# A gated mix of a state-space convolution and linear attention: its last attention output block emitted in two steps, and a new table for the order of all work

## The chip, the cores and the metric

The kernel runs on one core of a Trainium2 chip. The metric is device time in microseconds (us), the median of three runs: 252.57 us before the change (251.17 to 252.98). The engines are named as the profile names them: PE (TensorE, matrix products into PSUM), DVE (VectorE), ACT (ScalarE), POOL (GpSimd) and SP (SyncE, which here only issues transfers). "SPq" and "ACTq" are the queues of transfers that SP and ACT issue.

## The reference

One input x (2048 tokens of 512 channels) goes through two branches and is mixed by a gate:

```python
x = A_u
g = sigmoid((x * gate_w).sum(-1, keepdims=True))
a = _A_ref(x, ...)      # long convolution of each channel with a kernel K of 2048 taps, + u * Dskip
b = _B_ref(x, ...)      # 32 heads of 16; phi = [softmax(p), softmax(-p)] of q and k; linear attention; @ wo
return g * a + (1 - g) * b
```

K of branch a is the real part of a sum over 128 complex exponentials of each channel, K[d,l] = Re sum_n C[d,n] exp(dt A[d,n] l) dt B[d,n]. The convolution is a product of spectra (FFT of 4096 points). In branch b, kv sums phi_k times v over all tokens, z sums phi_k, and the output is (phi_q kv) / (phi_q z + 1e-6), times wo. The result is 2048 by 512 in bf16.

## The kernel before, in words

The kernel doesn't emit instructions directly. It records some thousand *nodes* (`P.add(engine, name, function, deps, ...)`, and `P.dma` for transfers), and `Plan.run` then emits them in the order of a table, `ORDER`: two base-64 digits for each node. Every engine executes its instructions in the order in which they were emitted, so the table sets the order on each engine. Three other tables go with it: `SIDES` says for each copy out of PSUM that may run on ACT or DVE which of them does it, `RINGS` from which of two PSUM pools a matmul's result takes its buffers (each of the big pools has two buffers), and `WARM`, `FOURS`, `ZPS` hold variants that the change leaves alone. A name in the text such as zk or kn is the name of a node. Transfers share eight completion semaphores: a transfer waits until the last one that used its semaphore has landed, whichever queue that was on.

The work has these stages, with the lines of the profile:

- Start. Weights and x are transposed on PE and copied out by ACT and DVE (xps to xT, wtp to wT, wps to WW and Wqp). The node p_e computes exp(log_dt) (ACT, `pt<-ld`, line 96), and the nodes p_t multiply parameters by it on DVE (`ppx<-psri`, line 347). The nodes udc copy x once more (`UDp<-UD`); the first stage of the input's FFT (psAu, line 517, its result copied by XAu) needs all four copies.
- Keys, eight rounds of two token tiles each: pk (PE, line 635) makes the keys, ek (ACT, `Ek<-pk`, line 96) two exponentials of each, zk (DVE, `Zk<-Ek`, line 662) their sums, rz (ACT, `Zk<-Zk` and `vr<-Zk`) the reciprocal as a logarithm and an exponential, vp (PE, line 683) the values, vb their copy out of PSUM, vr (DVE, line 692) the scaled values, and kn (PE, `kvp<-vr,Ek`, line 700) adds the round to kv. The FFT of the input (psAu and XAu, then psBu, line 542, and XU, `xst<-psB`) is woven into the rounds.
- Tables: between the rounds and after them DVE and ACT fill the tables of the exponentials (Ctab, Dtab), ACT with a sine table. argC (PE, `args<-selE,statC`, line 953) and cs (ACT, `cs<-args`) make the sines of four units at a time, argE and E the exponentials, El, Rh, Rl, A1, A2, A3 (DVE, lines 989, 1054, 1058, 1037, 1042, 1047) the factors of K of one unit (32 channels; sixteen units), and kps (PE, line 209) multiplies them. There is one buffer for A, so A1 of a unit waits for kps of the unit before.
- Queries (pq, eq, zs, z1 to z5, em, ops, oT, in four blocks of 512 tokens), woven into the units.
- The convolution of 128 channels at a time, then of 64, 32 and 32: psA and XA, psB and XK (FFT of K), t (DVE, line 1230, product of the spectra), psz and Zr (back), zw and zr (a turn through DRAM), psy (PE, line 1319) and ou (DVE, lines 1328 and 1330), which multiplies by the gate and writes into xT; from there the stores `out` (line 1341).
- The end: block 3 of the attention output, which adds the convolution's share Y, goes through bpsL (PE, lines 876 to 879), bs3 and bsg (copies, lines 177, 911 and 913) to the stores outL (line 925). bpsL makes two token tiles, k = 0 and 1, in one node:

Of the kernel before, what the change touches and what calls it, by code (L numbers as in the profile page):

```python
# [98 lines left out]
class Plan:  # L99

    DIGITS = "0123456789abcdefghijklmnopqrstuvwxyzABCDEFGHIJKLMNOPQRSTUVWXYZ-_"
    ORDER = ("0001021d0x0y0z0o0p0q0G0H0I0f0g0h0D0E0F170i0j0k181415162z2C0304051h2E0l0m0n0607082F0u0v0w2D0r0s0t2G2I2K1e1f090a0b1C2H0c0d"
             "0e1g2M1A1i1j1k0A0B0C1r2L2N2O2J1D1s102P11121t131L0-1E1u1v1w2S1M0_1B2Q2T2R1N1F1I0Y2U1b0Z1G2V1J191a2W0J0K0L0M0N0O0P0Q0R0S0T"
             "0U0V0W0X1c1S2X4n202Y2Z4u4v4w2A2-4x4J2_304y4K4L4M31324B4F4z4A4C1H4N344G4D334Q4E4H4I4Y1P4R364O354Z4U371K4P1R4S4-4V4_533839"
             "542B4T504W1X1O571Y4X513a525b3C585c3c5d5e59555i3b5j563d5a5f5q5r5g3h5m1U5s3i5h5t5k5x3D5n3j5o5l5u5y3e3f3g5B5p1Z5F5v5C3k5w3o"
             "5H5z5G5D5M5A5I3q1T5E215J3E3p5Q1V5R5K4o5N5L5U1Q3r3l3m3n4p1l1m1n5O1x1y1z1-5W3v3x5V5S3y5P3F1W3w5X5T67693G4q683I5Y6a3H6b3J5Z"
             "3K6c3M1o1p1q5-6d3L3N3s3t3u3O1_235_3P223Q3R25243S3U3T2b272d3V263W2c3z3A3B2f3X2h2e28632j2i3Y3Z3-3_402g2l412k43442s2u482942"
             "2t2m4a2n4b2o454647492p4f2q4c4d4e2w2r2v4h2a2x6064612y4i4g656e874r6i628b6f6j4j4k4l6g6686858a6k4m6h6l886r6m7x898c4s8d8e6t6q"
             "8h8i4t8j8f8n8g6u7y8k8l8B8o8t8p6v6w6s8C6-8m6x8q6y8u6_70718r9_8Y8Z8-8H6z8s6A6B72748v8D7z8Ia06n6o6p756C736D9293948w8K8E8F6E"
             "8L8x8y6F6G6H768M8G8z778Q787B8A7C8J6I6J6K8Ra8796M6N6O7a7A8N8Oa97b9R8P8S9Va19W6Laaa26P9S8T7D9X7c7d7e9U9Z8U6Qa5a36Sa68W8Vae"  # L110
             "a48X9Ta79Y6Tam7f7g7h9-6U6Ranaf7i6W7Eabac98as8_9091ad996X9a7F9g7Gag6V7n7H9h7Iao7j7k7lbSah7JbT7patavaw9b9i7K9596977m9c9j9k"
             "7L7M7Nap9o9paBaxbI9w9x6YaibMbNajakbJaqal6Z9q7r7O7P7QbO7S7T7U7oar7qauaC7RbL7sbQay9y7t7Waz9l9m9naA7YbK7u7vaD7ZaPaQaR7VbPb_"
             "7X7-bR7w80aEc0aMaNaOaFaHbYaG9r817_82bUbV9d9e9fc1bWbZbXaIaVc59s83aJaKaL9z84b1cm9t9u9vaWb-9AaXb2aYc6c2cnaSaTaUb9coaZdJc3ba"
             "cscddLdKc4ceb3ctbba-a_b0c7dM9B9C9DeFc8bhcgdNeGb4cfdO9E9F9Gb5cjbidPbcchdQdRbd9Kckcic9dS9Lewcbca9MclexeHcpdzccdDekelem9N9H"
             "9I9J9OdEcqbebfbgdCdHcrbjcubkdTdUdVcvblcwb6b7b89PcxeCcycAcBcCczdBeydWdXdY9QezcMeDd-d_e0dZeAcUeBcNcOe1cVbmbnbocDcEcFdAeEdF"
             "dGeIeLcPcWeJcGcHcIbpbqbreMd0d1eKdId2bvcXcQcYd8cJcKcLbwfld9eNcRcScTfmbxcZc-c_eOd3fGePd4dafobsbtbueRdbeQe2eSbyfndcfpeTe3bz"
             "fHeUe4e_e5freneoepf0fqbAfsd5d6d7dmbBdddedfeVeteuevdgdhdieWfMf1fteXfuf2fvdnfIf3fJdjdkdleYeZe-fNf4f5f6fKfLeqeresfwdpfxdqfy"
             "drdofOfPdsfQe6fRdtdudve7f7f8f9fSfTfafbfcfzeafAfUebe8fXdwdxdye9fBfVfYfWfCf-ecfdbCbDbEfZedbFbGbHg0fDfEfef_g1g2g3eeefegehei"
             "ejfffgfhfifjfkfFg4g5g6g7g8g9gagbgc")
# [1472 lines left out]
```

## Time and profile before

| | |
|---|---|
| median of three runs | 252.57 us |
| profiled execution, its own time | 253.07 us |
| its span (first to last instruction) | 251.3 us |
| DVE busy | 224.1 us (89%) |
| ACT busy | 210.7 us (84%) |
| PE busy | 203.6 us (81%) |
| mean share of the granted PE clock | 0.956 |

The profiled execution's own time is 1.8 us above its span, and 0.5 us above the median. In the views, a row of the timeline has the start, the duration, the engine, the line, the operation with `out<-in`, the shapes and how many instructions follow each other in that row; in square brackets stands the engine's idle time before the row and what ended it. Consecutive instructions of an engine overlap a little: DVE rows of 1.22 us follow each other every 1.13 us, ACT rows of 1.02 us every 0.91 us. In the view of windows each engine has its busy time and, in brackets, its instructions in the stretch; PEclk is the granted share of the PE clock.

### The profile page before, as it was taken

To read this page: it belongs to the slowest core of one execution; us is meant where nothing else is said; L and a number is where in the kernel's file an instruction comes from. 1 tells how busy PE (TensorE), PEld (TensorE's weight loads), DVE (VectorE), ACT (ScalarE), POOL (GpSimd) and SP (SyncE) were. 2 spreads that over 40 slices of the span, in tenths; PEclk is the share of its full clock that TensorE was granted. 3 is DMA by queue.
4 is the path that set the end of the run, shared out by engine and by line. 5 is a ranking of instruction groups with operands and counts; after the bars stand their busy time and mean duration, and the time that the engine had idled before them with its cause. 6 is when DMAs were issued, how large, how long until landed. Compare 5 with 4: busy or idle time off the path is not lost.

```text
span 251.3 us, 9877 instructions
## 1 busy us (share of the span) xinstructions
PE 203.6 (81%) x4437; PEld 141.7 (56%) x4437; DVE 224.1 (89%) x287; ACT 210.7 (84%) x291; POOL 2.4 (1%) x7
## 2 busy tenths in 40 slices
...
GB/s 132 262 180 195 411 12 4 109 106 118 84 222 0 170 210 288 93 3 23 180 69 202 60 50 223 284 3 125 172 208 195 199 208 231 246 191 140 209 181 92
DMA packets 61922, 38.23 MB, mean 152 GB/s; under 512 B 40632, under 2 KB 57272, under 8 KB 61496
## 3 DMA queue, kind: packets, MB, share of 16 engines
...
HBM read 24.49 MB, written 13.11 MB: 150 GB/s over the span
## 4 chain that ended last, share of the span: by engine, by line
ACT 30%; PE 28%; DVE 22%; DMA 11%; issue 5%; SPq 2%; ACTq 0%; DVEq 0%
ACT cs L96 6%; PE pk L635 4%; ACT Eq L96 4%; PE vp L683 4%; DMA Zd<-Zr 3%; PE psB L542 3%; ACT E L96 3%; DVE t L1230 2%; DMA wqk<-in_B_wqkv_dram 2%; ACT XA L175 2%; ACT L93 2%; DMA XUd<-xst 2%; PE kps L209 2%; DMA ax<-apd 2%; DMA ZT<-Zd 2%
## 5 line engine op out<-in xcount | busy, mean ns | idle before, releaser
L209 PE MATMUL kps<-R,A 128*32 128x64 bf16 x1664 | 30.5, 228 | 2.7 <-DVE A L1042 0.8
L209 PEld LDWEIGHTS <-A 128*32 128x32 bf16 x1664 | 28.6, 160 | 7.3 <-issue 3.9
L96 ACT ACTIVATE cs<-args 128x1024 bf16<-128x1024 f32 x32 | 30.7, 1054 | 0.0
L1058 DVE TENSOR_TENSOR R<-E,cs 128x2048 bf16<-128x2048 bf16 x16 | 19.5, 1217 | 0.0
L1037 DVE TENSOR_TENSOR A<-Ctab,Dtab 128x2048 bf16<-128x2048 bf16 x16 | 19.5, 1218 | 0.0
L1042 DVE TENSOR_TENSOR A<-Ctab,Dtab 128x2048 bf16<-128x2048 bf16 x16 | 19.5, 1217 | 0.0
L1054 DVE TENSOR_TENSOR R<-E,cs 128x2048 bf16<-128x2048 bf16 x16 | 19.5, 1217 | 0.0
L175 ACT CAST Zr<-psz 128x1024 bf16<-128x1024 f32 (+1 forms) x17 | 16.5, 974 | 3.2 <-issue 1.2
L175 ACT CAST XK<-psB 128x1024 bf16<-128x1024 f32 (+1 forms) x15 | 15.0, 1009 | 4.3 <-PE psB L222 2.8
L542 PE MATMUL psB<-XAu,TB 64*128 64x128 bf16 x256 | 12.8, 262 | 6.9 <-ACT xst L175 4.8
L175 ACT CAST XA<-psA 128x1024 bf16<-128x1024 f32 (+1 forms) x16 | 15.6, 1006 | 3.2 <-PE psA L216 3.2
L683 PE MATMUL vp<-WW,xT 128*128 128x512 bf16 x64 | 18.0, 411 | 0.0
L1230 DVE TENSOR_TENSOR t<-XUX,XK 128x2048 bf16<-128x2048 bf16 x14 | 17.1, 1218 | 1.0 <-ACT XK L175 1.0
L96 ACT ACTIVATE Ek<-pk 128x512 bf16<-128x512 f32 x32 | 16.9, 601 | 0.4 <-PE pk L635 0.2
L96 ACT ACTIVATE Eq<-pq 128x512 bf16<-128x512 f32 (+1 forms) x28 | 16.7, 710 | 0.2 <-PE pq L769 0.2
L96 ACT ACTIVATE E<-args 128x1024 bf16<-128x1024 f32 x16 | 16.8, 1057 | 0.0
L542 PEld LDWEIGHTS <-TB 64*128 64x128 bf16 x256 | 10.3, 116 | 11.0 <-issue 10.8
L1256 PE MATMUL psz<-t,small 128*128 128x512 bf16 x60 | 15.2, 380 | 1.6 <-ACT cs L96 0.5
L769 PE MATMUL pq<-xT,Wqp 128*128 128x512 bf16 x64 | 15.6, 380 | 0.6 <-ACT Eq L96 0.6
L635 PE MATMUL pk<-WW,xT 128*128 128x512 bf16 x64 | 16.0, 380 | 0.0
L662 DVE TENSOR_REDUCE Zk<-Ek 128x64 f32<-128x1024 bf16 x12 | 14.0, 1208 | 0.0
L222 PE MATMUL psB<-XA,TB 128*128 128x128 bf16 (+2 forms) x160 | 9.6, 205 | 4.3 <-ACT XA L175 1.4
...
## 6 DMA issues: line engine op xcount, KB each, us to landing
...
```

The costliest lines, as they stand in the source:

```text
L96: return self.nc.scalar.activation(**kw)
L175: self.nc.scalar.copy(out=o, in_=i)
L209: nc.tensor.matmul(kps[32 * dj:32 * dj + 32, g4, e, :], lhsT=A[:, ka, :, :, d].rearrange("p a b -> p (a b)"), rhs=R[:, kr, d, :], start=(i ...
L542: nc.tensor.matmul(box.ps[:, c2, sl, :], lhsT=fc.TB[rows, b0:b0 + 2].rearrange("p a b -> p (a b)"), rhs=X.t[rows, k, r0 + sl].rearrange("p ...
L635: nc.tensor.matmul(box.ps[:], lhsT=xT[:, st, kt, :], rhs=g.WW[:, kt, :], start=(kt == 0), stop=(kt == 3))
L683: nc.tensor.matmul(box.ps[:], lhsT=xT[:, st, kt, :], rhs=g.WW[:, 4 + kt, :], start=(kt == 0), stop=(kt == 3))
L769: nc.tensor.matmul(box.ps[:, m - m0, :] if late else box.ps[:], lhsT=g.Wqp[:, kt, 128 * m:128 * m + 128], rhs=xT[:, 4 * b:4 * b + 4, kt, : ...
L1037: nc.vector.tensor_tensor(out=c.A[:, 0:2].rearrange("p o a b c -> p (o a) b c"), in0=g.C[U // 8][:, 0:2, :, d0 % 256:d0 % 256 + 32].rearra ...
L1042: nc.vector.tensor_tensor(out=c.A[:, 2:4].rearrange("p o a b c -> p (o a) b c"), in0=g.C[U // 8][:, 1:3, :, d0 % 256:d0 % 256 + 32].rearra ...
L1054: nc.vector.tensor_tensor(out=c.R[:, :, :, 32:64], in0=t.E[:, 1].unsqueeze(1).to_broadcast([128, 2, 32, 32]), in1=t.cs[:], op=ALU.mult)
L1058: nc.vector.tensor_tensor(out=c.R[:, :, :, 0:32], in0=t.E[:, 0].unsqueeze(1).to_broadcast([128, 2, 32, 32]), in1=t.cs[:, ::-1, :, ::-1], o ...
L1230: nc.vector.tensor_tensor(out=box.t, in0=Ls[r0 // ns].X[:], in1=box.XK[:].unsqueeze(1).to_broadcast([128, 2, 1024]), op=ALU.mult)
```

## The change

bpsL of the last block becomes two nodes, bpsL for k = 0 and bpsM for k = 1, and bs3 and bsg depend on both. Nothing is added to or taken from the instructions: bpsM stands directly behind bpsL in the new order on PE. `SIDES`, `RINGS` and `ORDER` are replaced. The order differs not only in the last units but from the seventh digit of the table on.

```diff
     ORDER = (
-        "0001021d0x0y0z0o0p0q0G0H0I0f0g0h0D0E0F170i0j0k181415162z2C0304051h2E0l0m0n..."
+        "0001020x0y0z0o0p0q0G0H0I0f0g0h0D0E0F170i0j0k181415162z2C0304052E0l0m0n..."
...
-            def pbl(ip=ip, j=j, box=box):
-                box.ps = psum([128, 2, 512], "bps")
-                for k in range(2):
-                    out_mm(box.ps[:, k], 2 * ip + k, j + k)
+            def pbl(k, ip=ip, j=j, box=box):
+                if k == 0:
+                    box.ps = psum([128, 2, 512], "bps")
+                out_mm(box.ps[:, k], 2 * ip + k, j + k)
...
-            pb = P.add("PE", "bpsL", pbl, [ot[ip], pb, wo] + list(yn), take=[psq], rw=("diagD", ""))
-            e = P.add(("ACT", "DVE"), "bs3", lambda b3=b3: P.copy(*b3()), [pb] + g.xTr)
+            pb = P.add("PE", "bpsL", lambda pbl=pbl: pbl(0), [ot[ip], pb, wo] + list(yn), take=[psq], rw=("diagD", ""))
+            pm = P.add("PE", "bpsM", lambda pbl=pbl: pbl(1), [pb], rw=("diagD", ""))
+            e = P.add(("ACT", "DVE"), "bs3", lambda b3=b3: P.copy(*b3()), [pb, pm] + g.xTr)
             out.append(e)
             for k in range(2):
-                e = P.add(("ACT", "DVE"), "bsg", lambda k=k, bg=bg: bg(k), [pb, e, g.gate[0]], drop=(["psum"] if k else []))
+                e = P.add(("ACT", "DVE"), "bsg", lambda k=k, bg=bg: bg(k), [pb, pm, e, g.gate[0]], drop=(["psum"] if k else []))
```

Three places of the order, before and after. The first is the start of ACT's queue; `pt<-ld` is p_e, the exponential for which the first p_t on DVE waits. Before:

```order
L96 ACTIVATE dtc<-vecs 128x4
L96 ACTIVATE pt_127<-ld 128x512
L175 COPY wT_217<-wtp 128x1024 x2
L175 CAST WW<-wps 128x1024
L175 CAST Wqp<-wps 128x1024
L175 COPY xT<-xps 128x1024 x3
```

and after:

```order
L96 ACTIVATE dtc<-vecs 128x4
L175 COPY wT_207<-wtp 128x1024 x2
L175 CAST WW<-wps 128x1024
L175 CAST Wqp<-wps 128x1024
L175 COPY xT<-xps 128x1024 x2
L96 ACTIVATE pt_304<-ld 128x512
L175 COPY xT<-xps 128x1024
```

p_e moved from ahead of six copies out of PSUM to behind them. On DVE the order of the p_t nodes stays, and the last two UDp copies move behind the xT copy that follows them.

The second place is DVE in the first key rounds (`Zk` is zk, `vb` and `vr` the values of the round, `XAu` the copy of the FFT's first stage, `vr` the operand of kn). Before:

```order
L177 CAST XAu<-psA 128x256x4
L662 TENSOR_REDUCE Zk<-Ek 128x64 x2
L177 CAST vb<-vp 128x512
L346 TENSOR_TENSOR pt_126<-pmag,ppy 128x512
L692 TENSOR_TENSOR vr<-vb,vr 128x2x512 x2
L662 TENSOR_REDUCE Zk<-Ek 128x64 x2
L177 CAST XAu<-psA 128x256x4
L346 TENSOR_TENSOR pt_126<-pmag,ppx 128x512
L692 TENSOR_TENSOR vr<-vb,vr 128x2x512
```

and after:

```order
L177 CAST XAu<-psA 128x256x4
L177 CAST vb<-vp 128x512
L662 TENSOR_REDUCE Zk<-Ek 128x64 x2
L692 TENSOR_TENSOR vr<-vb,vr 128x2x512 x2
L177 CAST XAu<-psA 128x256x4
L177 CAST vb<-vp 128x512
L662 TENSOR_REDUCE Zk<-Ek 128x64 x2
L692 TENSOR_TENSOR vr<-vb,vr 128x2x512
```

Before, each zk stands directly behind the vr of the round before, and other work stands between zk and its own vr. After, the copies stand ahead of zk and the vr directly behind it. On PE the order of the first rounds becomes psAu, four pk, then four psAu and the first vp (before, psAu and pk alternated), and from the second round on kn, kn, pk, pk, psAu, vp. On ACT the first eight `Ek<-pk` stand ahead of the second and third XAu.

The third place is DVE at the start of the end, from the product of the spectra of the last 128-channel group on (XK, KD, Zr and oT are copies out of PSUM). Before:

```order
L1230 TENSOR_TENSOR t<-XUX,XK 128x2048
L1330 TENSOR_TENSOR xT<-psy,gT 128x8x128
L1230 TENSOR_TENSOR t<-XUX,XK 128x2048
L1037 TENSOR_TENSOR A<-Ctab_73,Dtab 128x2048
L989 TENSOR_TENSOR E<-E,Gtab 128x1024
L1042 TENSOR_TENSOR A<-Ctab_73,Dtab 128x2048
```

and after (its lines are one higher):

```order
L1231 TENSOR_TENSOR t<-XUX,XK 128x2048
L177 CAST XK<-psB 128x1024
L1331 TENSOR_TENSOR xT<-psy,gT 128x8x128
L177 CAST KD<-kps 128x1024
L177 CAST Zr<-psz 128x2x8x64
L1231 TENSOR_TENSOR t<-XUX,XK 128x2048
L1038 TENSOR_TENSOR A<-Ctab_73,Dtab 128x2048
L990 TENSOR_TENSOR E<-E,Gtab 128x1024
L177 CAST Zr<-psz 128x2x8x64
L1043 TENSOR_TENSOR A<-Ctab_73,Dtab 128x2048
L177 CAST oT_4973<-ops 128x1024
```

Five copies of 128x1024 out of PSUM moved from ACT to DVE. Later in the end the last Y and two bsg move to DVE as well, and one KD, one XAb, one bs3 and one bsg from DVE to ACT.

Other moves that the prediction speaks of: on PE the first four argC stand behind the last kn (before, the first of them stood between the last two vp), and on DVE the copy zrow (line 620) moves ahead of A1 and A2 of the first unit; kps of the sixth unit (PE, line 209) moves from ahead of the first two psz to behind them; two of the four outL stores move from ACT's queue to SP's, and the four store nodes after them (two for ou of 64 channels and two for the last two ou of 32, two of the four on each queue before and after) each change to the other queue.

More of the change, by code (lines that the diff above doesn't have):

```diff
@@ L101 @@
     DIGITS = "0123456789abcdefghijklmnopqrstuvwxyzABCDEFGHIJKLMNOPQRSTUVWXYZ-_"
[L102 to L106, printed above, removed]
-             "3K6c3M1o1p1q5-6d3L3N3s3t3u3O1_235_3P223Q3R25243S3U3T2b272d3V263W2c3z3A3B2f3X2h2e28632j2i3Y3Z3-3_402g2l412k43442s2u482942"
[L108 to L119, printed above, removed]
@@ new lines @@
+    ORDER = ("0001020x0y0z0o0p0q0G0H0I0f0g0h0D0E0F170i0j0k181415162z2C0304052E0l0m0n0607082F0u0v0w2D0r0s0t2G2I2K1e1f090a0b2H0c0d0e1g2M"
+             "1A0A0B0C2L2N2O2J102P1112131L0-1h1d1C1i1j1k1r1D1s1t1E2S1M0_1B2Q2T2R1N1F1I0Y1b0Z1G1J191a1c4n2U2V2W4u4v4w4x0J0K0L0M0N0O0P0Q"
+             "0R4y4J4K4L4M0S0T0U0V0W0X1S2X202Y2Z2A2-2_3031324B4F4C344G334z4A4D4Q4E4H4I4Y4Z4-4_1P4R36354U371R4V4N504O4P4S533839542B4T4W"
+             "1O574X5b5c5d5e3a3C583c5f515259555i3b5j563d5a5q5r5s5t3h5m1U3i5g5h5k5x3D5n3j5o5l5y3e3f3g5B5p5F5u5H5G5I5C3k3o5v5w5z5D5M5A3q"
+             "1T5E213E1u1v1w1H1K1X1Y1Z3p5Q1V5R4o5N5U1Q3r5J3l3m3n4p1l1m1n1x1y1z1-5W3v3x5V3y3F1W3w5X5K5L5O5S5P5T67693G4q683I5Y6a3H6b3J5Z"
+             "3K6c3M1o1p1q5-6d3L3N3s3t3u3O1_235_3P223Q3R25243S3U3T2b272d3V263W2c3z3A3B2f3X2h2e28632j2i3Y3Z3-3_402g2l412k43442s2u482942"
+             "2t2m2n2o2p2q2w2r2v2a2x4a4b454647494f4c4d4e4h4i4g4j4k4l606461656e4r6i626f6j6g666k6h6l6m2y878b86858a88898c4s4m6q8d4t6r7x8e"
+             "6t8h8i8j8f8n8g6u7y8k8l8B8o8t8p6v6w6s8C6-8m8q8r6x6y8u6_70719_8H72748D7z8Ia08s6n6o6p75738v8E8F8w8K8L8x8y8Y8Z8-6z6A6B6C6D92"
+             "93946E6F6G6H768G8M8z778Q787B8A7C6I6J6K8R8J8N8Oa8796M6N6O7a7Aa97b9R8P9Va19W6Laa8Sa2a36P9S8T7D9X7c7d7e9U9Z8U6Qa56Sa68W8Vae"
+             "a48X9T9Y6Tam7f7g7h9-6U6Ranaf7i6W7Ea7abac98adas8_9091996X9a7F9g7G6V7n7H9h7Iao7j7k7lbS7JbT7patavaw9b9i7K9596977m9c9j9kagap"
+             "aqah7L7M7N9o9paBaxbI9w9x6YaibMbNajakbJal6Z9q7r7O7P7QbO7S7T7U7o7qaC7RbL7sbQarauayaz9y7t7W9l9m9n7YbK7u7v7Z7V7X7-aA7w80817_"
+             "8283aPaQaRbPb_bRc0aMaNaObYaDaEaFaHaG9rbUbV9d9e9fc1bWbZbX84aIaVc59saJaKaL9zb1cm9t9u9vaWb-c2c39AaXb2aYc6cnaSaTaUb9coaZdJba"
+             "cscddLdKceb3ctc4bba-a_b0dM9B9C9DeHbhc7c8cgdNeIb4cfdO9E9F9Gb5cjbidPbcchdQdRbd9Kckcic9dS9Leycbca9MclcpcqcrezeJdzccdDemeneo"
+             "9N9H9I9J9OdEbebfbgdCdHbjbkdTdUdVblb6b7b89PeEcAcBcCdBeAcueBeCeDcvcwcxcyczdWdXdY9QcMeFd-d_e0dZcUcNcOe1cVbmbnbocDcEcFdAdFdG"
+             "eGeKeNcPcWeLcGcHcIbpbqbreOd0d1eMdId2bvcXcQcYd8cJcKcLbwfnd9ePcRcScTfobxcZc-c_eQd3fIeRd4dafqbsbtbueTdbeSe2eUbyfpdcfreVe3bz"
+             "fJbAeWe4f1e5ftepeqerf2fsfueXbBd5d6d7dmdddedfevewexf3fKfvfLfwdgdhdifOfPeYeZfxfyf4fMfNdjdkdldne-e_f0f5f6f7f8dpfzdqeseteufQ"
+             "drdsdofAfRfSe6e7e8fTebecfUfVe9eaedeefBfCfWfZf-f9fafbfcfdfebFbGbHbCbDbEdwdxdyefdtdudvfDfEegeheifXfYf_g0g2g1fFg3ejekelg4ff"
+             "fgfhfifjfkflfmfGg5fHg6g7g8g9gagbgcgdge")
```

6 lines of the change are left out of this document (3 added, 3 removed).

## The prediction

> **What bounds the kernel now.** I read the busy line of the page first, then the view of windows cut at the stages, then the timelines of DVE, ACT and PE beside each other. The windows show the stretch of the key rounds (26.3 to 65.7), the tables (to 99), the units (to 229.5) and the end; the columns behind the stretch are PE, PE's weight loads, DVE, ACT and POOL, then the clock of PE and the DMA share.
>
> ```profile
> PE 203.6 (81%) x4437; PEld 141.7 (56%) x4437; DVE 224.1 (89%) x287; ACT 210.7 (84%) x291; POOL 2.4 (1%) x7
> ```
>
> ```profile
> 26.30:65.70 39.40, 39.25 (x721) 22.72 (x720) 37.83 (x52) 38.19 (x74) 0.00 (x0) 1.00 0.36 114
> 65.70:99.00 33.30, 23.21 (x331) 15.29 (x330) 31.40 (x58) 31.61 (x39) 0.00 (x0) 0.74 0.55 163
> 99.00:229.50 130.50, 113.05 (x2848) 81.82 (x2847) 128.28 (x136) 123.07 (x158) 0.00 (x0) 1.00 0.58 150
> 229.50:245.50 16.00, 13.89 (x383) 8.95 (x383) 12.38 (x19) 6.28 (x10) 0.00 (x0) 1.00 0.73 185
> ```
>
> In the key rounds PE, DVE and ACT are all full: 39.25, 37.83 and 38.19 of 39.40 us. From 99 to 229.5 DVE works 128.28 of 130.50 us. So nearly every microsecond by which an engine is made to wait ahead of 229.5 comes out at the end; only the 2.2 us that DVE idles in the units and 3.6 us in the end can swallow any. The kernel is fast because of how its order interleaves, and the order is what the change replaces.
>
> **The split itself.** bpsM stands right behind bpsL on PE, and bs3 and bsg wait for both: the same matmuls and copies in the same place. 0 us.
>
> **The start: +4.6.** In the rows below, p_e (`pt<-ld`) is done at 13.40 on ACT, and DVE takes its first `ppx<-psri` at 18.16, with no idle time ahead of it.
>
> ```profile
> 12.77 0.63 ACT L96 ACTIVATE pt<-ld 128x512 f32<-128x512 bf16 x1 [3.55 <-DMA ld<-in_A_log_dt_dram]
> ...
> 19.89 2.89 ACT L175 COPY xT<-xps 128x1024 bf16<-128x1024 bf16 x3
> ```
>
> ```profile
> 18.16 0.68 DVE L347 TENSOR_TENSOR ppx<-psri,pt 128x512 f32<-128x512 f32 x1
> ...
> 24.70 0.42 DVE L177 COPY UDp<-UD 128x1024 bf16<-128x1024 bf16 x1
> 25.03 0.68 DVE L347 TENSOR_TENSOR ppx<-psri,ppx 128x512 f32<-128x512 f32 x1
> 25.73 0.69 DVE L177 COPY xT<-xps 128x1024 bf16<-128x1024 bf16 x1
> 26.34 1.22 DVE L177 CAST XAu<-psA 128x1024 bf16<-128x1024 f32 x1
> ```
>
> Now p_e stands behind the first two of the three xT copies: it starts at 21.7 and ends at 22.35. DVE, in order, waits 4.2 us. From 18.16 to 25.73 it worked 7.57 us almost without a gap; two UDp copies (some 0.34 each) leave this stretch, so xT ends at about 29.6, and the two UDp behind it end at 30.3. The first psAu needs all UDp, takes 0.60, and XAu starts at 30.9 in place of 26.34.
>
> **To the first vr: +4.7.** The next rows are DVE and PE in the first rounds, and ACT's Ek and rz (`Zk<-Zk` and `vr<-Zk`).
>
> ```profile
> 30.21 2.33 DVE L662 TENSOR_REDUCE Zk<-Ek 128x64 f32<-128x1024 bf16 x2
> 32.46 0.68 DVE L177 CAST vb<-vp 128x512 bf16<-128x512 f32 x1
> 33.06 0.68 DVE L346 TENSOR_TENSOR pt<-pmag,ppy 128x512 bf16<-128x512 f32 x1
> 33.66 1.28 DVE L692 TENSOR_TENSOR vr<-vb,vr 128x1024 bf16<-128x1024 bf16 x2
> 34.87 2.33 DVE L662 TENSOR_REDUCE Zk<-Ek 128x64 f32<-128x1024 bf16 x2
> 37.12 1.21 DVE L177 CAST XAu<-psA 128x1024 bf16<-128x1024 f32 x1
> 38.25 0.68 DVE L346 TENSOR_TENSOR pt<-pmag,ppx 128x512 bf16<-128x512 f32 x1
> 38.85 0.68 DVE L692 TENSOR_TENSOR vr<-vb,vr 128x1024 bf16<-128x1024 bf16 x1
> ```
>
> ```profile
> 34.40 1.06 PE L700 MATMUL kvp<-vr,Ek 128*32 128x34 bf16 x64
> 35.39 1.04 PE L635 MATMUL pk<-WW,xT 128*128 128x512 bf16 x4
> 36.26 0.60 PE L517 MATMUL psA<-small,UDp 128*128 128x256 bf16 x4
> ```
>
> ```profile
> 27.61 3.11 ACT L96 ACTIVATE Ek<-pk 128x512 bf16<-128x512 f32 x6
> ...
> 32.80 0.34 ACT L96 ACTIVATE Zk<-Zk 128x128 f32<-128x128 f32 x1
> 33.17 0.31 ACT L96 ACTIVATE vr<-Zk 128x128 bf16<-128x128 f32 x1
> ```
>
> Four pk now stand between the first psAu and the second, and on ACT eight Ek (8 times 0.51, 4.1 us) and an exponential (0.6) ahead of its XAu: from the first pk's end at 31.7 that XAu runs from 36.4 to 37.4. The fourth psAu needs the PSUM buffer it frees (there are two). Then two psAu at 0.44 apart and vp (as pk, 1.04) end at 39.3, vb at 40.0, zk (2.33) at 42.3, rz (0.65) at 43.0. There vr starts, against 33.66: 9.3 late, 4.6 of it told above.
>
> **The rounds: +17.5.** Before, a round is 33.66 to 38.85, 5.2 us: while ACT makes rz, DVE has XAu or a pt to do, and zk stands ahead of both copies. After, DVE has XAu, vb, zk, vr, each waiting for the one before, and on PE the psAu that XAu waits for stands behind kn, which waits for vr. Nothing fills the waits. One turn of this ring: vr twice 0.60 and 0.68, kn of the second tile 0.45, two pk 1.89, psAu 0.60, XAu 1.22, vb 0.68, zk 2.33, rz 0.65: 9.1 us, 3.9 more than before. Five rounds (the second to the sixth) have this form; in the later ones the copy in the ring is xst behind psB, of much the same size, or only vb behind vp (9.1 - 0.60 - 1.22 + 1.04 = 8.3, so +3.1). I take 3.5 each, 17.5; with 3.1 or 4.5 in all it is 15.5 or 22.5. The lower bound, if the engines still find work in the waits, is nothing for this term.
>
> **The tables: +3.3.** The rows are the last kn, the first cs and, on DVE, the first E.
>
> ```profile
> 95.78 0.89 PE L700 MATMUL kvp<-vr,Ek 128*32 128x34 bf16 x64
> ```
>
> ```profile
> 93.41 7.50 ACT L96 ACTIVATE cs<-args 128x1024 bf16<-128x1024 f32 x8
> ```
>
> ```profile
> 103.27 0.69 DVE L989 TENSOR_TENSOR E<-E,Gtab 128x1024 bf16<-128x1024 bf16 x1 [0.17 <-ACT E L96]
> ```
>
> The argC for which cs waits stood ahead of the last kn; now they all stand behind it, so cs starts at 96.75 (95.78 + 0.89, and the first argument) and not at 93.41, and E, for which DVE waited already, follows. Between 0, if the last key round is not late itself, and 4.2 with the zrow copy, which now holds DVE ahead of A1 and A2.
>
> **The units: +3.5.** kps of the sixth unit moves from ahead of two psz to behind them.
>
> ```profile
> 144.40 1.22 DVE L1230 TENSOR_TENSOR t<-XUX,XK 128x2048 bf16<-128x2048 bf16 x1
> ...
> 146.67 1.22 DVE L1037 TENSOR_TENSOR A<-Ctab,Dtab 128x2048 bf16<-128x2048 bf16 x1
> ```
>
> ```profile
> 140.61 2.24 PE L209 MATMUL kps<-R,A 128*32 128x64 bf16 x128
> ```
>
> The second psz waits for this t, which ends at 145.62; a psz of about one microsecond and kps (2.24) behind it end at 148.9. The next unit's A1, at 146.67 before, needs the one buffer of A that kps reads: +2.2. The same move at the twelfth kps I put at 1.3, by the same rows with more slack. From 0 (the idle time of other engines covers it) to 5.
>
> **The end: +2.8.** Five copies go from ACT to DVE, 1.13 each (the XAu row, less the overlap): 5.65 on an engine that is busy up to 229.5. In the end DVE idles 3.6 of 16 us; with the copies that go to ACT (1.8) against those that come (1.7) I let it regain half of that, 1.7 or so. The last store then gains:
>
> ```profile
> 245.03 0.42 DVE L1330 TENSOR_TENSOR xT<-psy,gT 128x256 bf16<-128x256 f32 x1 [0.40 <-PE psy L1319]
> ```
>
> ```profile
> 245.79 2.93 SPq L1341 DMA_DIRECT2D out_dram<-xT  x4
> ```
>
> The last ou ends at 245.45, and SP still issues four stores, about 0.73 apart, the last at some 248. With two outL on SP in place of ACT, the store of 64 channels goes out on both queues ahead of the last ou, and the last issue is at about 246.5: -1.6. A wait for the copies' matmuls, 0.5, makes up the rest: 5.65 + 0.5 - 1.7 - 1.6 = 2.8. Bounds: -1.6 (the copies covered) and +6.2.
>
> "Trainium Kernel Development and Optimization" of the Trainium skill, section "Key Constraints", says that transfers from several queues run on the same 16 DMA engines, and that more issuing engines only save the sequencer's issue time; by it the store term would be two issues of the row above, 1.5, and the trace, where the last four issues follow each other without a gap, agrees.
>
> **The sum.** 4.6 + 4.7 + 17.5 + 3.3 + 3.5 + 2.8 = 36.4; the 2.2 us that DVE idles in the units takes up 2 of it. Against the profiled execution's own 253.07 that gives 287.5; this execution is 0.5 above the median of 252.57, so 287.
>
> **The rivals.** (a) The ring is looser than I read it, and ACT, DVE and PE find each other's work in the rounds, so that half of the 17.5 or all of it falls away, and the later terms hide in the tables. Against it: each engine is in order, and the rows above show no engine that has slack to run ahead. For it: my walk takes each queue's row as waiting for the slowest input. The start and the first vr remain: 253 + 9.3 = 262, with half of the rounds 271. (b) PE's clock falls in the thinner head. The windows show 0.74 where PE is busy 23.21 of 33.30 us (70%), and 1.00 where it is full. After, 39.25 us of PE work lie in about 62 us, 63%. At half the clock the ring's 2.94 us on PE (kn, pk, psAu) double; in about three of five rounds that is +8.8, 296. "TensorE: Matmul & The Clock Gate" of the Trainium skill, section "Part 1: The HAM clock gate (the "warmup" mystery)", puts the gate at half speed after an idle window of about 3.4 us and at full after as long a busy one. By it a ring whose wait on DVE and ACT is 5.6 us long could drop each turn; the 0.74 of the tables agrees that the clock falls with waits, but no row shows it within the rounds. (c) The other side: the end is bound by ACT, not DVE, so that ACT's shedding of five copies (0.91 each, 4.6) and the stores' 1.6 are a gain, 6.2: 246.8. It decides only if start, rounds and tables together cost less than 6.2, against the 9.3 up to the first vr; DVE's 12.38 busy of 16 against ACT's 6.28 in the end speak against it. (d) The engines take the moves up and nothing comes out: 252, by the 2.2 and 3.6 us of idle time only if the head's delay were under these.
>
> **How the numbers follow.** The forecast (272 to 292) has 0.58, (a) 0.20, (b) 0.13, (c) 0.05, (d) 0.04. The likeliest gives 287. From the bounds of the rounds (15.5 to 22.5), the tables (0 to 4.2), the units (0 to 5) and the end (-1.6 to 6.2) the forecast alone could lie further out, but not all at once. The range takes in most of (a) and all of (b): 266 to 300, and leaves out (c), (d) and the lower part of (a). One per cent is about what a measurement of this kernel tells from no change. Slower is forecast, (a) and (b): 0.91; within 1% (d): 0.04; faster (c): 0.05.
>
> **What would show it.** The start: `ppx<-psri` on DVE at 22.4 behind 4 us of idle time put down to ACT, and XAu at 30.9. The first vr at 43. The rounds: DVE's busy share in them down from 96% to some 65%, its waits put down to PE's psA and to ACT's vr, the last XAu of the input's FFT some 27 us later. Tables: cs directly behind the last kn. The units: A1 with idle time behind kps after the sixth unit. The end: DVE with five copies of 1.1 us around t, the last issue under 1.5 us behind the last ou. If the first vr comes before 38, or rounds take under 7 us, the forecast is wrong, and the time falls to (a) or below.

## The result, and the profile after

The changed kernel takes 336.3 us (median of six runs, 335.0 to 339.0) against 251.66 us (six runs, 250.4 to 253.0): ratio 1.336, 95% interval 1.330 to 1.341. It is 84.6 us slower. The direction was forecast; the size, +34, was not, and 336 lies far outside the range of 266 to 300. Now and then an execution of one of these kernels takes over 1.5% longer than its others, at a lower granted clock, and the times and ratios below leave such executions out.

The busy times of the page, and the view of windows, cut at the same events as before (first XAu to ninth XAu, to the first A1, to the last ou of 128 channels, to the last ou):

```profile
PE 228.8 (68%) x4437; PEld 151.5 (45%) x4437; DVE 231.6 (69%) x291; ACT 209.7 (63%) x287; POOL 2.4 (1%) x7
```

```profile
30.45:100.15 69.70, 48.98 (x722) 25.97 (x721) 38.70 (x50) 39.57 (x74) 0.00 (x0) 0.83 0.23 63
100.15:141.40 41.25, 25.51 (x342) 15.70 (x341) 31.97 (x58) 34.22 (x41) 0.00 (x0) 0.70 0.38 115
141.40:312.40 171.00, 125.14 (x2875) 87.61 (x2873) 134.66 (x141) 119.32 (x151) 0.00 (x0) 0.88 0.44 110
312.40:326.00 13.60, 13.07 (x344) 7.91 (x344) 11.66 (x18) 5.18 (x10) 0.00 (x0) 1.00 0.56 154
```

DVE and ACT do nearly the same work in each stretch as before; what grew is the time in which they wait. In the key rounds DVE now works 38.70 of 69.70 us (before 37.83 of 39.40), in the units 134.66 of 171.00 (before 128.28 of 130.50). PE is 25 us busier in all with the same 4437 matmuls, at a granted clock of 0.83 in the rounds and 0.88 in the units, where it was 1.00 (0.852 in the mean of the execution, 0.956 before).

The longest entries of the view of waits (in total, times, longest) tell who waits for whom:

```profile
DVE A L1038 <- PE kps L209: 30.4, 10, 6.6
PEld L700 <- issue: 22.2, 16, 6.4
ACT Ek L96 <- PE pk L635: 19.8, 12, 3.7
PE kvp L700 <- DVE vr L692: 19.1, 7, 6.4
DVE XAu L177 <- PE psA L517: 12.3, 4, 4.2
```

Three of them are the ring of the key rounds (kn for vr, XAu for psA, Ek for pk). The first is in the units and as large as all that the prediction gave to the head. The view of waits of the kernel before has no wait of A1 for kps.

Where the time came from, by the start of the same node in both traces: the first XAu is 4.1 us late, the first vr 9.8, the ninth XAu 34.5, the first A1 42.5, the first kps 42.1, the fourteenth A1 76.2, the last ou 81.0.

### The profile page after: what moved, and what is told of

Read it like the earlier page. It is cut to its first block, busy times and chain, and to the rows that moved or that the text cites. A ratio compares the mean times of both kernels' runs of the same rounds, so it can differ in the third digit from the quotient of the medians.

```text
span 334.5 us, 9876 instructions
## 1 busy us (share of the span) xinstructions
PE 228.8 (68%) x4437; PEld 151.5 (45%) x4437; DVE 231.6 (69%) x291; ACT 209.7 (63%) x287; POOL 2.4 (1%) x7
## 4 chain that ended last, share of the span: by engine, by line
PE 35%; ACT 25%; DVE 23%; issue 8%; SPq 4%; DMA 3%; DVEq 0%; ACTq 0%
PE kps L209 6%; PE pk L635 6%; ACT cs L96 6%; PE psz L1257 4%; PE pq L769 3%; DVE t L1231 3%; DVE vr L692 3%; DMA UD<-in_A_u_dram 3%; SPq L1466 2%; DVE Zk L662 2%; ACT xst L175 2%; ACT XA L175 2%; ACT E L96 2%; PE psB L542 2%; ACT trg L96 2%
## 5 line engine op out<-in xcount | busy, mean ns | idle before, releaser
L209 PE MATMUL kps<-R,A 128*32 128x64 bf16 x1664 | 30.1, 234 | 5.0 <-DVE A L1048 1.6
L1257 PE MATMUL psz<-t,small 128*128 128x512 bf16 x60 | 19.4, 458 | 11.5 <-DVE t L1231 6.4
L635 PE MATMUL pk<-WW,xT 128*128 128x512 bf16 x64 | 22.0, 511 | 0.0
L175 ACT CAST Zr<-psz 128x1024 bf16<-128x1024 f32 (+1 forms) x15 | 14.2, 961 | 10.7 <-PE psz L1257 5.3
L700 PE MATMUL kvp<-vr,Ek 128*32 128x34 bf16 x512 | 6.9, 200 | 19.5 <-DVE vr L692 19.1
L683 PE MATMUL vp<-WW,xT 128*128 128x512 bf16 x64 | 19.6, 444 | 0.7 <-ACT vb L175 0.7
L769 PE MATMUL pq<-xT,Wqp 128*128 128x512 bf16 x64 | 18.4, 430 | 1.1 <-ACT Eq L96 1.1
L692 DVE TENSOR_TENSOR vr<-vb,vr 128x1024 bf16<-128x1024 bf16 x16 | 10.5, 688 | 11.3 <-ACT vr L96 9.1
L175 ACT CAST XK<-psB 128x1024 bf16<-128x1024 f32 (+1 forms) x14 | 13.8, 991 | 6.5 <-PE psB L222 6.5
L177 DVE CAST XAu<-psA 128x1024 bf16<-128x1024 f32 x7 | 8.4, 1220 | 12.3 <-PE psA L517 12.3
```

The source lines that it names most:

```text
L175: self.nc.scalar.copy(out=o, in_=i)
L209: nc.tensor.matmul(kps[32 * dj:32 * dj + 32, g4, e, :], lhsT=A[:, ka, :, :, d].rearrange("p a b -> p (a b)"), rhs=R[:, kr, d, :], start=(i ...
L635: nc.tensor.matmul(box.ps[:], lhsT=xT[:, st, kt, :], rhs=g.WW[:, kt, :], start=(kt == 0), stop=(kt == 3))
L683: nc.tensor.matmul(box.ps[:], lhsT=xT[:, st, kt, :], rhs=g.WW[:, 4 + kt, :], start=(kt == 0), stop=(kt == 3))
L692: nc.vector.tensor_tensor(out=K.v[:, u, :, 0:16, :], in0=box.v[:].unsqueeze(1).to_broadcast([128, 2, 16, 32]), in1=K.v[:, u, :, 16:17, :]. ...
L769: nc.tensor.matmul(box.ps[:, m - m0, :] if late else box.ps[:], lhsT=g.Wqp[:, kt, 128 * m:128 * m + 128], rhs=xT[:, 4 * b:4 * b + 4, kt, : ...
```

## The experiments

Up to entry 440 and up to entry 860 the two tables hold the same sets of nodes; 440 is at the first kps, 860 at the tables of the last two units. So pieces of the tables can be joined. In the diffs, B is the order of before with bpsM put behind its bpsL, A the new one, and the engines and PSUM pools of each node go with the piece it is in.

**The split alone.**

```diff
-ORDER = A
+ORDER = B        # with B's engines and queues
```

> The kernel before with bpsL cut into bpsL and bpsM and nothing else; the order, engines and queues are those of before. Prediction's step: 0 us, since bpsM stands right behind bpsL and both copies wait for both. Rival: the second node brings a wait or a semaphore of its own on PE, +0.5 to +2 us.

251.81 against 251.82 us, ratio 1.0009 (0.9968 to 1.0051). The split costs nothing that can be measured, as forecast. Its trace has another use: its A1 of the sixteenth unit starts 2.1 us earlier than that of the kernel before, its first A1 only 0.4, with the same order of all work. So two profiled executions of one order can differ by 1.6 us in the units.

**Head, middle and end apart.**

```diff
+head_new: ORDER = A[0:440] + B[440:]
+mid_new:  ORDER = B[0:440] + A[440:860] + B[860:]
+end_new:  ORDER = B[0:860] + A[860:]
```

> The new order and engines up to the first kps (start, key rounds, tables), the order of before from there. Prediction's sum for these stages: 4.6 + 4.7 + 17.5 + 3.3 = +30, so about 282 us. If the stages are independent and the trace of the changed kernel shows each stage's own loss, +42 (the first kps is 42.1 us later there), about 294 us. Rival: the rest of the kernel takes part of the lateness up, under +25.

> The order of before up to the first kps and again from the tables of the last units on; the new order of the units between. Prediction's term: +3.5, so about 256 us. Theory from the trace of the changed kernel: this stretch loses on its own, +34 (76.2 - 42.1), about 286 us. Rival: it loses there only because the late and cold head puts it out of step; then under +10.

> The order of before up to the tables of the last units; the new order, engines and store queues from there, with the split. This is the part that the change's words describe. Prediction's term: +2.8, bounds -1.6 to +6.2. From the shifts of the changed kernel in its end (76.2 to 81 at the last ou, 84.7 at the last store): +5 to +8.5. Rival (c) of the prediction: the shed copies and shared stores gain, -1 to -6.

| | us | ratio to before (95%) | over 251.82 |
|---|---|---|---|
| head_new | 292.08 | 1.161 (1.153 to 1.169) | 40.3 |
| mid_new | 285.45 | 1.135 (1.127 to 1.142) | 33.6 |
| end_new | 259.35 | 1.031 (1.026 to 1.036) | 7.5 |

Together 81.4 of the 84.6 us. The three stretches lose on their own account: the middle loses as much behind the head of before as behind a late one. The kernels that follow were each timed beside the kernel before, and their losses are against those times (251.1 to 252.2 us). end_new, which is what the change's words describe, is itself 3% slower; the other nine tenths come from a table that is new everywhere.

**Head: new up to the fifth round.**

```diff
-ORDER = A[0:440] + B[440:]
+ORDER = A up to kn of round 5, then the rest in the order of B
```

> The new order only up to kn of the fifth round, the order of before from there. The trace of the changed kernel puts +9.8 on the way to the first vr, +14.2 on rounds 1 to 5 (3.5 each, the prediction's figure), +9.7 on the sixth round alone and +7.7 on the tables. If that is where the head's 40.3 us lie, this kernel loses 23 to 25, about 276 us, and 16 of the 40 come back against head_new. Rival: the sixth round and the tables are long only because PE came into them cold and late; then they are long here too, and it stays above 285 us.

276.49 us, 24.3 above before (ratio 1.094, 1.087 to 1.101). So the way to the first vr and rounds 2 to 5 cost 24 us, and the sixth round with the tables the other 16 of 40.3. In this kernel's trace the sixth round, in the old order behind five new ones, takes 7.4 us from vr to vr, so it isn't the late and cold head that makes it long. The rows of DVE and PE in the changed kernel's sixth round show what is there (columns: start, duration, then the idle time ahead in brackets):

```profile
78.92 1.30 DVE L692 TENSOR_TENSOR vr<-vb,vr 128x1024 bf16<-128x1024 bf16 x2 [4.65 <-ACT vr L96]
...
81.67 2.35 DVE L177 CAST xst<-psB 128x1024 bf16<-128x1024 f32 x2
84.72 0.17 DVE L600 TENSOR_SCALAR gz<-gps 128x16 f32<-128x16 f32 x1 [0.70 <-PE gps L596]
89.05 1.23 DVE L177 CAST xst<-psB 128x1024 bf16<-128x1024 f32 x1 [4.15 <-PE psB L542]
90.19 0.42 DVE L177 COPY UDp<-UD 128x1024 bf16<-128x1024 bf16 x1
90.52 1.22 DVE L177 CAST xst<-psB 128x1024 bf16<-128x1024 f32 x1
91.66 2.33 DVE L662 TENSOR_REDUCE Zk<-Ek 128x64 f32<-128x1024 bf16 x2
94.70 1.29 DVE L692 TENSOR_TENSOR vr<-vb,vr 128x1024 bf16<-128x1024 bf16 x2 [0.71 <-ACT vr L96]
```

```profile
82.94 1.74 PE L596 MATMUL gps<-vecs,xT 128*128 128x1 bf16 x64 [0.93 <-DVE xst L177]
84.55 2.64 PE L635 MATMUL pk<-WW,xT 128*128 128x512 bf16 x8
87.12 1.89 PE L542 MATMUL psB<-XAu,TB 64*128 64x128 bf16 x32
...
95.45 0.45 PE L700 MATMUL kvp<-vr,Ek 128*32 128x34 bf16 x32 [6.45 <-DVE vr L692]
```

From vr to vr this round takes 15.8 us (before 54.87 to 61.02, 6.2), 9.6 more. One chain holds it all: xst on DVE frees the buffer for gps, behind gps stand two pk and two psB on PE, behind those the last two xst on DVE, and behind them zk, rz and vr. Rounds 2 to 5, 43.41 to 78.92, took 35.5 us against 21.2: 3.6 more each in the mean, and 5.1, 2.3, 3.0 and 3.9 one by one.

**Head: zk early.**

```diff
  vr vr                 # DVE, end of a round (rounds 1 to 3 and 5)
+ zk
  XAu / UDp / xst ... vb
- zk
  vr vr
```

> As head_new, but zk of rounds 2, 3, 4 and 6 stands directly behind the vr of the round before on DVE, as in the order of before, not behind the copies. Ring theory (the prediction's step on the rounds): zk (2.33 us) leaves the ring in four rounds, -9 us, about 283 us. Rival: the rounds are bound by PE at its lower clock, not by the ring; no change, 291 to 293 us.

288.35 us (287.8 and 288.9), 37.2 above before, where head_new is 40.3 above; ratio to before 1.149 (1.141 to 1.157). In its trace the first kps is 5.3 us earlier than in head_new; rounds 2 to 5 give 4.8 of it, the sixth 0.8: vr there stands behind the last two xst in any case. The ring theory holds in direction; four times 2.33 was too much. The third round gains nothing, and the sixth isn't this ring; in the second, rz on ACT stands behind a copy and an exponential, and vr waits 1.8 us for it.

**Head: PE kept busy.**

```diff
 def kn(u, st, K):
+    for _ in range({0: 10, 2: 14, 4: 4, 6: 10, 8: 10, 10: 26}.get(st, 0)):
+        matmul(unread columns of the kv bank, lhsT=ident, rhs=240 columns of small, start=False)
```

> As head_new, with extra matmuls of 240 columns on PE ahead of the kn at which PE waits for vr (10, 14, 4, 10, 10 and 26 of them), written into columns of the kv bank that nothing reads. Theory of the prediction's rival (b): the waits lower PE's clock (0.82 in the rounds), and pk, vp and psA, which stand in the ring, take up to twice their time; PE is 9.6 us busier than before between 30.4 and 100. Kept busy, PE holds its clock and some 5 to 9 us come back, 283 to 287 us. Rival: the clock isn't on the path; no change, or slower by the extra matmuls that don't fit in the waits.

294.68 us (293.5 and 295.8), 43.6 above before, where head_new is 40.3 above. The windows from the first psAu to the ninth XAu, head_new first, then this kernel:

```profile
30.40:100.00 69.60, 48.86 (x723) 25.86 (x721) 38.71 (x50) 39.58 (x74) 0.00 (x0) 0.83 0.24 63
```

```profile
30.40:95.40 65.00, 52.09 (x800) 31.73 (x798) 38.70 (x51) 39.20 (x74) 0.00 (x0) 0.93 0.25 67
```

The clock rises from 0.83 to 0.93, the stretch is 4.6 us shorter though PE has 74 matmuls more to do in it, and the first kps is 5.0 us earlier. So the clock is on the path of the rounds, for about 5 us there. Rounds 2 to 5 take 31.3 us in this kernel, 2.5 more each than before, where head_new has 35.4. But the total is not better: by the last ou the lead is gone. In the units, where nothing was changed, the lead shrinks by 1 to 2 us at a time at kps, with waits of PE there that the view of waits puts down to "issue" (four, 4.0 us in all; head_new has none in that row). What causes them is not shown, so the gain in the whole time stays unproved.

**Head: p_e early.**

```diff
  dtc
+ p_e
  wTe wTe wpe wpe xT xT     # ACT
- p_e
  xT
```

> As head_new, with p_e (exp of log_dt) back ahead of the copies on ACT. Prediction's term for the start: 4.6, so -4.1 to -4.6, about 288 us. Rival: the first rounds wait for something else anyway (the four pk and eight Ek), and less than 2 us come back.

291.4 us (291.0 to 295.0), ratio to before 1.165 (1.153 to 1.177), where head_new has 1.161: no gain that can be told from none. Here the rival was right. The changed kernel's DVE at the start:

```profile
21.82 0.69 DVE L347 TENSOR_TENSOR ppx<-psri,pt 128x512 f32<-128x512 f32 x1 [4.17 <-ACT pt L96]
...
28.34 0.68 DVE L177 COPY xT<-xps 128x1024 bf16<-128x1024 bf16 x1
28.94 0.75 DVE L177 COPY UDp<-UD 128x1024 bf16<-128x1024 bf16 x2
30.45 1.22 DVE L177 CAST XAu<-psA 128x1024 bf16<-128x1024 f32 x1 [0.76 <-PE psA L517]
```

The 4.17 us of waiting for p_e are as forecast. Without them, though, the first psAu starts only 1.8 us earlier (27.99 for 29.79): xT waits 2.02 us for its transposes, these for a transfer of x that has landed by 25.5, and the last two UDp stand behind that xT, as in the new order. XAu starts at 29.09, so with p_e in its old place 2.7 of the start's 4.1 us remain. The place of UDp alone, with p_e late, wasn't tried. In the trace the lead is 3.2 us at the first kps and 1.3 at the last ou.

**Middle: two kps.** On PE the new order of the units differs from the old in little more than where kps stands: the kps of units 2, 5, 6, 7, 8, 10 and 12 come later. mid_seg takes the new order for units 5 to 7 alone, kps5_late moves one kps.

```diff
  argC                  # PE, mid_seg (kps5_late: unit 5 only)
- kps (unit 5)
  argE ops ops
+ kps (unit 5)
  psB128 zs psB128
- kps (unit 6)
  ops argE ops argE psz psz
+ kps (unit 6)
```

> The order of before, but the new order in the stretch of units 5 to 7 alone. On PE just two things differ there: kps of unit 5 stands behind three more matmul groups (arguments and two ops), kps of unit 6 behind six (ops, arguments, two psz); with it the copy KD of unit 6's pair stands behind the two Zr copies on ACT, and A2 or A3 of units 5 to 7 one place earlier on DVE. Theory from the trace of mid_new: +5 for unit 5 and +6 for unit 6, +10 to +13 in all (A1 of unit 5 is 5.2 us late there, A1 of unit 8 17.7), about 262 us. Rival, the prediction's own step: +2.2 for unit 6 and nothing for unit 5, about 254 us; then the loss of the middle needs the whole new order.

> The order of before, with one move: on PE, kps of unit 5 stands behind three groups (one of arguments, two ops) that it stood ahead of. The prediction gave this move no cost. Theory from mid_seg: kps starts 3.1 us later there and A1 of unit 6 2.2 us, so +1.5 to +2.5 us, and the rest of mid_seg's 8.9 is the move of unit 6's kps with KD. Rival: a single late kps is taken up by the order of before, under +0.7.

mid_seg: 260.92 us (259.6 and 262.3), 9.0 above before (ratio 1.036, 1.028 to 1.045). kps5_late: 253.62, ratio 1.0073 (1.0034 to 1.0112), which is 0.9 to 2.8 us: a single late kps isn't free. The one wait of A1 in its trace, at unit 6, says where:

```profile
141.71 1.23 DVE L1038 TENSOR_TENSOR A<-Ctab,Dtab 128x2048 bf16<-128x2048 bf16 x1 [1.95 <-PE kps L209]
```

Against the split's trace A1 falls back by 2.0 us there, and by the last unit 1.8 of it is left. mid_seg has three such waits of A1 for kps, 1.91, 5.98 and 0.91 us, 8.8 together, which is what the kernel loses. PE and DVE of mid_seg at the longest, kps of unit 6 and A1 of unit 7:

```profile
147.72 1.86 PE L1257 MATMUL psz<-t,small 128*128 128x512 bf16 x4 [1.56 <-ACT E L96]
150.69 1.87 PE L1257 MATMUL psz<-t,small 128*128 128x512 bf16 x4 [1.10 <-ACT Zr L175]
152.48 2.27 PE L209 MATMUL kps<-R,A 128*32 128x64 bf16 x128
```

```profile
154.80 1.23 DVE L1038 TENSOR_TENSOR A<-Ctab,Dtab 128x2048 bf16<-128x2048 bf16 x1 [5.98 <-PE kps L209]
```

The prediction held this very move to cost 2.2 us: t at 145.62, "a psz of about one microsecond", kps. In fact each psz takes 1.86 here (eight matmuls took 1.94 before) at a granted clock of 0.50 between 147.7 and 152.5, and each psz waits for ACT first: one for E (psz doesn't read E; presumably it waits for the PSUM buffer that E frees), one for Zr. A1 waits 5.98 us. And the prediction counted two such moves, where the table has seven. In the changed kernel the time from the last factor's end to the start of kps is 7.2, 5.3, 11.3, 7.4, 9.5 and 7.3 us for units 3, 5, 6, 7, 8 and 10 (in unit 3 nothing passed kps; pq ahead of it came late); before, no unit has more than 2.2. Its A1 of unit 7, and PE's rows ahead of it, are the same picture:

```profile
199.41 1.87 PE L1257 MATMUL psz<-t,small 128*128 128x512 bf16 x4 [1.10 <-ACT Zr L175]
201.21 2.28 PE L209 MATMUL kps<-R,A 128*32 128x64 bf16 x128
```

```profile
203.54 1.22 DVE L1038 TENSOR_TENSOR A<-Ctab,Dtab 128x2048 bf16<-128x2048 bf16 x1 [5.99 <-PE kps L209]
```

**Middle: kps early.**

```diff
  A3                    # mid_new, units 3, 5, 6, 8, 10, 12, 13
+ kps
  pq / ops / argE / zs / psz / bpsq / psB ...    # PE
- kps
```

> As mid_new, but on PE kps of units 3, 5, 6, 8, 10, 12 and 13 moved ahead of the work (pq, ops, zs, psz, bpsq, arguments, psB) that stands between its factors and it; DVE and ACT keep the new order. Theory: the units lose their time because kps waits in PE's queue behind work of other chains, and A1 of the next unit then waits on DVE for the one buffer of A (in mid_new kps starts up to 11.3 us after its factors are done, before at most 2.2). Then more than half of the 33.6 us comes back, under 268 us. Rival: late kps is a symptom, and the moved work becomes late in its place (psz, ops); then it stays above 277 us.

It is slower, not faster: 291.4 us. The profile is of an execution of 298.1 us, so its waits tell where they are better than how long. The waits, mid_new first:

```profile
DVE A L1038 <- PE kps L209: 31.0, 10, 6.0
```

```profile
DVE A L1038 <- PE kps L209: 14.6, 7, 4.1
ACT cs L96 <- PE args L954: 11.2, 6, 5.1
```

A1's wait is halved, and ACT's cs waits for arguments that now come late. That fits the rival: the work that was moved back became late in turn. Moving kps as early as its factors allow goes further than the order of before, in which part of that work stands ahead of it. So the middle is shown in part. In mid_new's trace A1 falls back, against before, by 5 to 7 us at each of units 4, 6, 7, 9 and 11, and at each it waits for kps (at unit 4 for 1.9 us only); for the moved kps of units 5 and 6 the two kernels above show the cause. For the others, and for unit 3, whose kps wasn't moved, the place of the loss is shown, but not that moving kps alone makes it: the new order of the units with each kps exactly in its old place, or with a second buffer of A, wasn't tried.

**End: copies.**

```diff
-XK KD Zr Zr oT on DVE        # end_new
+XK KD Zr Zr oT on ACT
```

> As end_new, with the five copies (XK, KD, two Zr, oT) on ACT again, in the new order. Prediction's step: five copies of 1.13 us cost DVE 5.65, of which the end regains 1.7, so -4 against end_new, about 255 us. Trace of end_new: the last ou is 4.1 us late, so -4 at most. Rival: the new order of the end costs the time, not the engines; less than 1 us comes back.

254.36 us (ratio 1.010, 1.004 to 1.017), 2.5 above before and 5.0 below end_new. This term was right to about a microsecond: 5.65 less 1.7 had been forecast, 4. The copies in the changed kernel's DVE, at 1.13 each:

```profile
290.09 1.21 DVE L177 CAST KD<-kps 128x1024 bf16<-128x1024 f32 x1
291.22 1.21 DVE L177 CAST Zr<-psz 128x1024 bf16<-128x1024 f32 x1
```

**End: stores.** Five kernels. end_stores and end_cs bring back queues and sequence of the stores (end_cs with the five copies on ACT), end_q the queues alone (with the copies on ACT too), outL_sp moves one pair of outL to SP in the kernel before, zt_first puts the last ZT loads ahead of the stores there.

```diff
 end_new, SP:   ZT ZT out#2 out#1 out#4 out#3 outL#1 out#5 out#7   ACT: outL#2 out#6 out#8
+end_cs, SP:    out#3 ZT ZT out#4 out#1 out#2 out#6 out#8          ACT: outL#1 outL#2 out#5 out#7
+end_stores, SP: out#3 out#4 out#1 out#2 ZT ZT out#6 out#8         ACT: outL#1 outL#2 out#5 out#7
+end_q, SP:     ZT ZT out#2 out#1 out#4 out#3 out#6 out#8          ACT: outL#1 outL#2 out#5 out#7
+outL_sp, SP:   out#3 ZT ZT out#4 out#1 out#2 outL#1 out#6 out#8   ACT: outL#2 out#5 out#7
+zt_first, SP:  ZT ZT out#3 out#4 out#1 out#2 out#6 out#8          ACT: outL#1 outL#2 out#5 out#7
```

> As end_new, with the stores out and outL on the queues and in the order of before. Prediction's step: the new queues save 1.6 us, so about 261 us here. Trace of end_new: SP's two stores of the 32-token rows wait 7 us for a completion semaphore that a store of ACT holds, and the last issue is 4.8 us behind the last ou in place of 3.1; so 1 to 3 us come back, about 257 us.

> The kernel before (with the split, which costs nothing), one outL store pair moved from ACT's queue to SP's and nothing else: the prediction's store term by itself. By that step -1.6 us, about 250 us, since SP's store of 64 channels then no longer waits until 245.8 for a semaphore of ACT's fourth outL. Rival: the transfers share what limits them, or the semaphore wait only moves; no change within 0.5 us.

> As end_copies (new order of the end, the five copies on ACT), with the stores out and outL on the queues of before and in their sequence of before, the loads of ZT between them as there. end_copies is 3.0 us above before, and its last ou only 0.4 us later than with the split alone: theory, these 3.0 are the stores, so 252 us, the time of before. Rival: the order of the end costs them, 255 us.

> As end_copies (new order of the end, five copies on ACT), with out and outL on the queues of before and the new sequence kept, so that the last ZT loads stand ahead of all stores on SP. end_copies loses 3.0 us, and in its trace all of it lies between the last ou (0.4 late) and the last issue of a store (5.4 us behind it, 2.8 with the split alone). Theory: the queue change costs these 2.5, and the time is that of before or up to 1 us better, 251 to 252.5. Rival: the new sequence costs them whichever queue, 255 us.

> The kernel before with the split, and one move on SP: the last four ZT loads stand ahead of the first store pair. In end_cs, where that store pair stands ahead of them, ZT lands late and the last four ou come some 3 us later than in end_copies; in the order of before it stands ahead of them too. Theory: -0.5 to -1.5 us, about 251. Rival: in the order of before ZT isn't waited for; no change within 0.4 us.

| | us | ratio to before (95%) |
|---|---|---|
| end_stores | 261.10 | 1.038 (1.033 to 1.044) |
| outL_sp | 252.69 | 1.0047 (1.0013 to 1.0081) |
| end_cs | 255.78 | 1.0127 (1.0078 to 1.0176) |
| end_q | 255.23 | 1.0098 (1.0060 to 1.0137) |
| zt_first | 253.59 | 1.0057 (1.0027 to 1.0088) |

end_stores came out where the prediction's step had it, but for another reason: its stores stand ahead of the last ZT loads, and ou of 64 channels is 4.3 us later than in end_new. It is no test of the queues. outL_sp is: the store term, -1.6 by the prediction, is +1.2 by itself (0.3 to 2.0, from the ratio). SP's queue there and in the split, with the last ou of each at 243.26 and 242.21, shows a wait for a semaphore: in outL_sp the store just ahead of the moved pair is issued at 242.71, when the store before it on SP had gone out at 237.07; the semaphore that it waits for was last used by an outL that ACT issued at 239.95. The last store issues at 247.03 in outL_sp, 3.8 us behind its ou, at 245.03 in the split, 2.8 behind. In end_copies too, the last store is issued late:

```profile
240.61 4.00 SPq L1342 DMA_DIRECT2D out_dram<-xT  x4
245.01 0.85 SPq L926 DMA_DIRECT2D out_dram<-xT  x2
245.96 2.67 SPq L1342 DMA_DIRECT2D out_dram<-xT  x4
```

The first four have 4.00 us from the first issue to the end of the last, and the outL and the last four follow them, so that the last issue is 5.4 us behind the last ou (242.63); in the split it is 2.8. That made the queues the suspect for the 2.5 us (0.9 to 4.2) that end_copies loses. In end_q, with the old queues, the last issue is 4.1 us behind the last ou, but the last four ou stand 1.6 us later behind the ou before them, and it takes 255.23 all the same. end_cs, for which 252 was forecast, takes 255.78. Its ZT loads land late behind a store pair, and so zt_first was to gain 0.5 to 1.5 by putting them ahead; it lost 0.7 to 2.2 instead, and its last four ou come 1.1 us later than in the split. Neither queues alone nor queues with sequence give the 2.5 us back. By elimination they lie in the new order of the end, with the engines and PSUM pools of its other copies; which move carries them stays open. None of these kernels was faster than the one before.

## Why the prediction was right or wrong

| step | forecast | trace of the changed kernel | run |
|---|---|---|---|
| split | 0 | | 0.0, with an interval of -0.8 to +1.3 |
| start | +4.6 | +4.1 | |
| to the first vr | +4.7 | +5.6 | |
| rounds | +17.5 | +24.7 | |
| tables | +3.3 | +8.0 | |
| these four | +30.1 | +42.5 | +40.3 |
| units | +3.5, less 2 | +33.7 | +33.6 |
| end | +2.8 | +7.0 (336.3 - 253.07 - 76.2) | +7.5 |

**Start and first vr**: right in size and place. p_t ran at 21.82 (22.4 forecast), XAu at 30.45 (30.9), vr at 43.41 (43.0). (By its own rows the sum ends xT 0.3 us too early, at 29.6 for 29.9.) As to cause, p_e accounts for less than half of the start: with p_e back, 2.7 of 4.1 us remain, behind xT and the two UDp, which the sum had as a detail.

**Rounds**: right in direction for four of five, and nearer in size than the argument earned. "I take 3.5 each" met 3.6 in the mean of rounds 2 to 5, but the ring was priced at full clock, and with PE kept busy the same rounds cost 2.5 each; about a third of the 3.6 is the clock, which the forecast had left to rival (b). That the two errors cancel is luck. The step that failed is "Five rounds (the second to the sixth) have this form": the sixth has another, with gps, two pk, two psB and two xst in one chain, and cost 9.6, not 3.5. Its moves were counted and not walked.

**Rival (b)**, PE's clock, had 0.13 and came true beside the forecast: 0.83 in the rounds, PE 48.98 us busy there for 39.25. Its 8.8 us were too many: keeping PE busy shortened the stretch by 4.6 us. That the gate falls with waits agrees with the page "TensorE: Matmul & The Clock Gate" of the Trainium skill, section "Part 1: The HAM clock gate (the "warmup" mystery)": its idle window of about 3.4 us is shorter than the longest waits of PE here (6.45 us), and the two pk behind that wait took 3.24 us (96.44 to 99.68), 1.9 before, with a granted clock of 0.50 from 95.4 to 99.1.

**Tables**: forecast 3.3, traced 8.0. The rows of ACT and DVE:

```profile
133.22 7.44 ACT L96 ACTIVATE cs<-args 128x1024 bf16<-128x1024 f32 x8 [4.63 <-PE args L954]
```

```profile
144.36 1.02 ACT L96 ACTIVATE E<-args 128x1024 bf16<-128x1024 f32 x1 [2.40 <-PE args L976]
```

```profile
140.82 0.69 DVE L620 TENSOR_SCALAR zrow<-zps 128x512 f32<-128x512 f32 x1 [5.78 <-PE zps L615]
141.43 1.22 DVE L1038 TENSOR_TENSOR A<-Ctab,Dtab 128x2048 bf16<-128x2048 bf16 x1
...
145.42 0.69 DVE L990 TENSOR_TENSOR E<-E,Gtab 128x1024 bf16<-128x1024 bf16 x1 [0.38 <-ACT E L96]
```

Two waits were named: cs behind the last kn, and zrow ahead of A1, which was left in the bound as 0.9 more. The last kn starts 35.8 us late, cs 39.8, A1 42.5, the first kps 42.1. So cs behind kn was nearly right, 4.0 for 3.3; 1.3 us more than at the ninth XAu were there by the last kn already. The zrow copy waits 5.78 us and makes A1 late, but it is not what E waits for: E on DVE waits for E on ACT, and this for its arguments, which stand on PE behind zps and two pq (3.29 us, 1.90 before). That wait of 2.40 us is the term that the sum didn't have.

**Units**: the step that failed, and the largest, 33.7 us for 3.5. The sum counted two of the seven moved kps, and priced the wait of A1 (+2.2) as if the psz ahead of kps could run at once and at full clock. At unit 6 the kernel mid_seg shows what stood there instead: two waits of psz for ACT, both psz at twice their time, and a wait of A1 of 5.98 us. With kps of unit 5, which had no term, that is 9.0 us; that the rest of the 33.7 has the same cause is argued from the same waits of A1 and not shown by a run. The 2 us of DVE's idle time that were to take up part of the lateness took up none that can be seen: head_new's units run 1.6 us shorter than those of the profiled execution of before, but so do the split's, with no late head ahead of them.

**End**: five copies, right to about a microsecond (5.0 for 4). The stores, wrong in sign: -1.6 was forecast, and moving one outL pair alone gives +1.2. The prediction counted issues on the two queues; it had no term for a store that waits for a semaphore of the other queue, and the 2.5 us of the end that stay open lie in no term of it.

**Rivals (a), (c) and (d)** are out: rounds didn't overlap, ACT's shedding of copies gained nothing (end_new is slower), and the order did change things.
